# Induced attention with a max-out layer: quadrant maxima exchanged through DRAM, and a running softmax in batches 1 to 3

## The chip, the core and the metric

The kernel runs on one core of a Trainium2 chip. A core has five engines with instruction streams of their own: TensorE (PE in the profile, its weight loads PEld), VectorE (DVE), ScalarE (ACT), GpSimd (POOL) and SyncE (SP, which issues all transfers here). They meet only at semaphores. The metric is the device time of one execution in microseconds, the median of several runs.

## The reference

Four batches of 12544 tokens with 128 channels go through two attentions with 32 inducing vectors, and then a max-out layer:

```python
    def mab(q, kv):
        s = scale * (q @ kv.transpose(0, 2, 1))
        s = s - s.max(-1, keepdims=True)
        a = np.exp(s)
        a /= a.sum(-1, keepdims=True) + 1e-09
        return a @ kv
    h = mab(I, x)                 # I: the 32 inducing vectors; h: 32 x 128 for a batch
    return mab(x, h)
    ...
    h = np.maximum(np.maximum(x @ w1, x @ w2), x @ w3)
    return (h @ w_out)
```

The first attention has 32 queries and 12544 keys: its softmax runs over all tokens of a batch, and its result `h` is needed before the second one can start on that batch.

## The kernel before

A batch's 98 tiles of 128 tokens are cut into 7 groups: group 0 with 2 tiles, groups 1 to 6 with 16 (2048 tokens). The second attention and the max-out layer work on chunks of 512 tokens, four to a full group; a chunk has six steps, one for each 128 of the 768 hidden columns. In a step, TensorE makes `pu` and `pv` (L606, L612) in `advance`, ScalarE makes the relu `ru` and the rounded `hi`, VectorE takes the maximum `h` of `pv` and `ru` (L639), GpSimd (for some steps VectorE, L642) makes the remainder `lo`, and, six steps later, `stage2` has TensorE add three products to `acc` (L662 to L664).

All engines are scheduled by hand: an instruction stands on its engine where the Python program issues it. `main` walks over the steps; in each it calls `advance`, loads the `pT` of a chunk two ahead (every sixth step), copies and stores a finished chunk, then runs what the table `plan` holds for the step, then `stage2`. `at(s, f, ...)` enters a function at step `s`. A window is the 24 steps of one group, and `s0` is its first step. `burst` enters products at `s0 + 2` and at `s0 + 15`.

While batch b goes through these windows, the first attention of batch n = b + 1 is done in between, one group at a time (batch 0's is done ahead of the steps, in `phase1_first`). For a group gi, `attend_products` (L263, in a burst) writes 32 scores for each token into a bank, the tokens spread over four quadrants of 32 partitions. So each quadrant has a maximum of its own (`mq`, L273), and the four must become one. Before, this takes three instructions: ScalarE writes `mq` into the columns of a 128x4 tile by a mask (`attend_column`, L280), TensorE multiplies it with the constant `sel` so that every partition has all four (`attend_spread`, L287), and VectorE takes the least of them (the maxima are kept negated; `attend_least`, L291) into `mneg`. Then ScalarE takes the exponentials (`attend_weights`, L297), VectorE transposes them (`attend_transpose`, L311), and in the next burst TensorE sums weighted tokens (`attend_sums`, L321) into the `acc` bank that the running chunk does not use, from where ScalarE copies them to `hg` (`attend_keep`, L334). `softmax1` enters these; its argument `wait` is `LATE` (12 steps) for groups 2 and 3.

Every group has its own maximum. At the batch's end (window 5, steps 10 to 18) the seven are joined: their least, the weights `w` of the groups, a mask `sw` (128 x 7 x 32) from `w` and `sel`, seven products of `hg` with the mask (`combine_groups`, L423), the sum of the exponentials by a product (`total_sums`, L439), its reciprocal, and `hT`, the result.

The tiles `xTs` (group 0) and `xT` hold transposed tokens for the score products; `load_channels` loads them on SP. SP works in order: a transfer whose data or buffer isn't ready holds up all that follow it.

Of the kernel before, what the change touches and what calls it, by code (L numbers as in the profile page):

```python
# [25 lines left out]
def kernel(ctx, tc, x, xt, ind_t, w1, w2, w3, w_out, out):  # L26
    nc = tc.nc
# [42 lines left out]
    op = ctx.enter_context(tc.tile_pool(name="op", bufs=2))  # L70
    ps = ctx.enter_context(tc.tile_pool(name="ps", bufs=1, space=PSUM))
# [152 lines left out]
    def start_batch(b):  # L224
        st = state[b] = {"xT": {}, "xg": {}, "a": {}, "s": {}}
        st["mneg"] = bp.tile([P, NG], F32, name="mneg", tag="mneg")
        st["lst"] = bp.tile([P, NG], F32, name="lst", tag="lst")
        st["hg"] = bp.tile([P, NG, C], F32, name="hg", tag="hg", bufs=1)
# [63 lines left out]

    def attend_weights(b, gi):
        w = groups[gi]["nt"] * M
        st = state[b]
        a = wk.tile([P, 512], F32, name="a", tag="a")
        nc.scalar.activation(  # L297
# [3 lines left out]
            bias=st["mneg"][:, gi : gi + 1],  # L301
            accum_out=st["lst"][:, gi : gi + 1],
        )
        st["a"][gi] = a
# [24 lines left out]
    def attend_keep(b, gi):  # L329
# [4 lines left out]
        nc.scalar.copy(out=st["hg"][:parts, gi, :], in_=st["h"][:parts, :C])  # L334

# [388 lines left out]
    for b in range(B):  # L724
        base = b * per_batch + short
        n = b + 1
        for g in range(1, NG):
# [7 lines left out]
            if n < B:  # L735

                if g == 1:
                    at(s0, start_batch, n)
                    at(s0, load_channels, n, 0)
                    at(s0, load_channels, n, 1)  # L740
                    if n == 1:
                        at(s0 + 1, load_tokens, 1, 4)
# [4 lines left out]
                    at(s0 + 16, attend_keep, n, 0)  # L747
# [3 lines left out]
                elif g < NG - 2:  # L751
                    first += [(attend_sums, n, g - 1), (attend_products, n, g, bank_a[1])]
                    at(s0 + 3, attend_keep, n, g - 1)
# [7 lines left out]
                    if g == NG - 3:  # L761
                        second += [(attend_sums, n, g), (attend_products, n, g + 1, bank_a[1])]
                        at(s0 + 16, attend_keep, n, g)
                        softmax1(n, g + 1, s0 + 15)
                        at(s0 + 16, load_tokens, n + 1, 2)
                elif g == NG - 2:
                    first += [(attend_sums, n, g), (attend_products, n, g + 1, bank_a[1])]
                    at(s0 + 3, attend_keep, n, g)
# [137 lines left out]
```

## Time and profile before

| What | Value |
|---|---|
| median of 3 runs | 843.36 us |
| lowest and highest run | 843.27 and 845.08 us |
| the profiled execution's span, first to last instruction | 841.7 us |
| what lies around it, to the median of the runs | 1.7 us |
| mean granted TensorE clock | 0.995 |
| busy share of the span | PE 97%, ACT 88%, DVE 75%, POOL 75% |

A row of the groups or of the timeline reads: line, engine, operation, tiles written <- read, shape, number of instructions. In the timeline the start and the length stand ahead, and in brackets the idle time of the engine before it with what ended it. Lengths of TensorE instructions are modelled and overlap; their starts are what counts. The span leaves out what the device does around the program, so that it can be a little under the time of a run; the page gives no other time for the profiled execution.

### The profile page before, as it was taken

The page shows a single profiled execution, that of the slowest core. Times are in us where ns is not written, and L with a number is a line of the kernel's source. Part 1 is how long each engine was busy: PE and PEld are TensorE (multiplying, and loading weights), DVE is VectorE, ACT ScalarE, POOL GpSimd, SP SyncE. Part 2 cuts the span into 40 slices and gives each one's busy share as a digit, 9 for nine tenths or more (in the row PEclk, how much of TensorE's full clock was granted, in tenths as well). Part 3 has the DMA queues.
Part 4 walks back from the last instruction along what each step waited for, and adds up shares of the span by engine and source line. Part 5 has one row for each costly group of instructions (what it writes and reads, how often), then busy time and mean ns, then how long its engine had stood idle before and what let it go on. Part 6 is the DMA issues. An engine that isn't in the chain of part 4 may idle for free.

```text
span 841.7 us, 14677 instructions
## 1 busy us (share of the span) xinstructions
PE 817.0 (97%) x4608; PEld 635.9 (76%) x4608; DVE 630.7 (75%) x1076; ACT 741.3 (88%) x1547; POOL 635.4 (75%) x512
## 2 busy tenths in 40 slices
PE   6879999999999999999999999999999999999998
PEld 4647778777787777777777777877768878778786
DVE  5868778777686777777787778777868778777864
ACT  5759889898798998988799889889879999999996
POOL 0039778778597787877778878878759888888887
PEclk9989999999999999999999999999999999999999
DMA  9734624433425345244332462432222222222221
GB/s 348 267 96 155 219 76 157 169 116 103 146 66 175 126 157 173 70 164 158 114 92 76 162 216 70 163 122 58 64 77 81 79 75 69 64 70 76 72 79 51
DMA packets 42717, 102.50 MB, mean 122 GB/s; under 512 B 8976, under 2 KB 11152, under 8 KB 37392
## 3 DMA queue, kind: packets, MB, share of 16 engines
q1 hardware_dynamic: 42640, 101.57, 37.3%
q8 instruction: 37, 0.61, 0.3%
q14 instruction: 40, 0.33, 0.1%
HBM read 48.12 MB, written 25.69 MB: 88 GB/s over the span
## 4 chain that ended last, share of the span: by engine, by line
PE 92%; DMA 3%; DVE 2%; ACT 1%; issue 1%; SPq 0%; ACTq 0%; DVEq 0%
PE acc L662 17%; PE acc L663 16%; PE acc L664 16%; PE pu L606 16%; PE pv L612 16%; PE acc L661 3%; PE aux L525 3%; PE acc L321 2%; DMA xg<-in_x_dram 2%; PE aux L263 2%; DMA xTs<-in_xt_dram 1%; PE aux L490 1%; PE aux L423 1%; ACT ru L621 0%; PE acc L287 0%
## 5 line engine op out<-in xcount | busy, mean ns | idle before, releaser
L636 POOL TENSOR_TENSOR lo<-h,hi 128x512 fp32r<-128x512 f32 (+1 forms) x498 | 629.5, 1296 | 153.6 <-ACT hi L628 100.5
L639 DVE TENSOR_TENSOR h<-pv,ru 128x512 f32<-128x512 f32 (+1 forms) x600 | 404.5, 675 | 188.0 <-PE pv L612 122.6
L621 ACT ACTIVATE ru<-pu 128x512 f32<-128x512 f32 (+1 forms) x600 | 375.8, 626 | 73.8 <-PE pu L606 70.7
L628 ACT CAST hi<-h 128x512 fp32r<-128x512 f32 (+1 forms) x600 | 386.9, 645 | 0.3 <-DVE h L639 0.3
L662 PE MATMUL acc<-hi,wo_hi 128*128 128x512 f32 (+1 forms) x600 | 238.4, 397 | 0.0
L606 PE MATMUL pu<-pT,us 128*128 128x512 f32 (+1 forms) x600 | 232.7, 388 | 3.4 <-ACT hi L628 1.2
L612 PE MATMUL pv<-pT,us 128*128 128x512 f32 (+1 forms) x600 | 233.4, 389 | 0.0
L663 PE MATMUL acc<-hi,wo_lo 128*128 128x512 f32 (+1 forms) x600 | 232.0, 387 | 0.0
L664 PE MATMUL acc<-lo,wo_hi 128*128 128x512 f32 (+1 forms) x600 | 231.8, 386 | 0.0
L662 PEld LDWEIGHTS acc<-hi,wo_hi 128*128 128x128 f32 x600 | 113.2, 189 | 43.0 <-issue 22.0
L606 PEld LDWEIGHTS pu<-pT,us 128*128 128x128 f32 x600 | 113.2, 189 | 26.9 <-POOL us L479 2.0
L612 PEld LDWEIGHTS pv<-pT,us 128*128 128x128 f32 x600 | 113.4, 189 | 23.8 <-DVE h L639 1.3
L664 PEld LDWEIGHTS acc<-lo,wo_hi 128*128 128x128 f32 x600 | 113.0, 188 | 23.0
L663 PEld LDWEIGHTS acc<-hi,wo_lo 128*128 128x128 f32 x600 | 113.3, 189 | 20.6
L642 DVE TENSOR_TENSOR lo<-h,hi 128x512 fp32r<-128x512 f32 x102 | 72.4, 710 | 0.8 <-ACT hi L628 0.8
L669 ACT COPY o<-acc 128x512 f32<-128x512 f32 (+1 forms) x100 | 61.6, 616 | 3.1 <-PE acc L664 3.1
L661 PE MATMUL acc<-pT,us 128*128 128x512 f32 (+1 forms) x100 | 38.7, 387 | 0.0
L321 PEld LDWEIGHTS acc<-xg,aT 128*32 128x32 f32 x768 | 20.5, 110 | 13.9 <-ACT ru L621 5.7
L219 POOL TENSOR_TENSOR wo_lo<-wf,wo_hi 128x768 fp32r<-128x768 f32 x1 | 1.8, 1809 | 37.5 <-ACT wo_hi L218 37.5
L263 PE MATMUL aux<-xT,iT 128*32 128x512 f32 x192 | 25.9, 596 | 1.6 <-ACT xT L255 1.6
L321 PE MATMUL acc<-xg,aT 128*32 128x128 f32 x768 | 25.8, 274 | 1.5 <-DVE aT L311 1.1
L525 PE MATMUL aux<-xT,hT 128*32 128x512 f32 x192 | 25.6, 604 | 0.0
(101 smaller groups left out, 438.6 us busy)
## 6 DMA issues: line engine op xcount, KB each, us to landing
out_dram<-o SPq DMA_DIRECT2D x96, 256.0 KB, 2.0
xg<-in_x_dram SPq DMA_DIRECT2D x23, 1024.0 KB, 7.3
xT<-in_xt_dram SPq DMA_DIRECT2D x18, 1024.0 KB, 5.3
pT<-ph SPq DMA_DIRECT2D x192, 64.0 KB, 2.0
pT<-pl SPq DMA_DIRECT2D x192, 64.0 KB, 2.0
raw<-in_w_dram SPq DMA_DIRECT2D x3, 768.0 KB, 12.0
us<-uh SPq DMA_DIRECT2D x6, 208.0 KB, 3.1
us<-ul SPq DMA_DIRECT2D x6, 208.0 KB, 3.7
```

The lines of the kernel that those rows point to most:

```text
L321: nc.tensor.matmul(out=hps[q * M : (q + 1) * M, :C], lhsT=aT[:, t * M : (t + 1) * M], rhs=xg[:, t, :], start=(t < NQ), stop=(t + NQ >= nt),)
L606: nc.tensor.matmul(out=pu[:, :w], lhsT=state[c.b]["us"][:, 2 * j * P : (2 * j + 1) * P], rhs=c.pT[:, :w], start=True, stop=True)
L612: nc.tensor.matmul(out=pv[:, : d.w], lhsT=state[d.b]["us"][:, (2 * j + 1) * P : (2 * j + 2) * P], rhs=d.pT[:, : d.w], start=True, stop=True,)
L621: nc.scalar.activation(out=ru[:, :w], in_=pu[:, :w], func=AF.Relu)
L628: nc.scalar.copy(out=hi[:, : c.w], in_=h[:, : c.w])
L636: nc.gpsimd.tensor_sub(**args)
L639: nc.vector.tensor_max(out=h[:, : d.w], in0=pv[:, : d.w], in1=relus.pop(s)[:, : d.w])
L642: nc.vector.tensor_sub(**low)
L661: nc.tensor.matmul(out=c.acc[:, :w], lhsT=us[:, 2 * DF :], rhs=c.pT[:, :w], start=True, stop=False)
L662: nc.tensor.matmul(out=c.acc[:, :w], lhsT=wo_hi[:, j, :], rhs=c.hh[j][:, :w], start=False, stop=False)
L663: nc.tensor.matmul(out=c.acc[:, :w], lhsT=wo_lo[:, j, :], rhs=c.hh[j][:, :w], start=False, stop=False)
L664: nc.tensor.matmul(out=c.acc[:, :w], lhsT=wo_hi[:, j, :], rhs=c.hl[j][:, :w], start=False, stop=(j == NJ - 1))
```

## The change

In batches 1 to 3 the four quadrants' maxima go through DRAM: `attend_send` writes `mq` to a small DRAM tile `mqd`, `attend_fetch` reads it back so that every partition has the four values of its inducing vector, in `mm`. `running_least` takes the least of these four and of the least so far. `attend_weights` uses that running maximum as its bias, and makes the factor `fac` by which what was summed before must shrink; `running_sums` keeps one running tile `hs` and one running sum `ls` on VectorE. At the end `running_totals` makes two products with `sel`, in place of the seven products and the mask. Everything from the exponentials on stands one step later in `softmax1`; the products and sums stay in their bursts. And `start_batch` and the first two loads of batches 2 and 3 move from the first step of the window in which they are used to steps 8 and 14 of the window before. Batch 0 stays as it was.

```diff
+    def attend_send(b):
+        st["md"] = dp.tile([P], F32, name="mqd", tag="mqd")
+        nc.sync.dma_start(out=st["md"].rearrange("(m q) -> q m", q=NQ), in_=st["mq"])
+    def attend_fetch(b, gi):
+        every = st["md"].rearrange("(m q) -> m q", q=NQ).unsqueeze(0).to_broadcast([NQ, M, NQ])
+        nc.sync.dma_start(out=st["mm"][:, gi, :NQ], in_=every)
+    def running_least(b, gi):
+        known = NQ + 1 if gi > 0 else NQ
+        nc.vector.tensor_reduce(
+            out=st["mm"][:, gi + 1, NQ:], in_=st["mm"][:, gi, :known], axis=AX.X, op=ALU.min
+        )
...
     def attend_weights(b, gi):
+        least = st["mneg"][:, gi : gi + 1] if b == 0 else st["mm"][:, gi + 1, NQ:]
...
+        if b > 0 and gi > 0:
+            nc.scalar.activation(
+                out=st["fac"][:, gi : gi + 1], in_=st["mm"][:, gi, NQ:], func=AF.Exp, bias=least, scale=-1.0
+            )
...
+    def running_sums(b, gi):
+        if gi == 0:
...
+            nc.vector.tensor_copy(out=st["hs"][:parts, :], in_=st["h"][:parts, :C])
+            return
+        nc.vector.scalar_tensor_tensor(
+            out=st["hs"], in0=st["hs"], scalar=fac, in1=st["h"][:, :C], op0=ALU.mult, op1=ALU.add
+        )
+        nc.vector.scalar_tensor_tensor(out=st["ls"], ...)   # the same for the sum of the exponentials
+    def running_totals(st, bank):
+        st["lp"], st["sum"] = bank[:, :M], bank[:, M : 2 * M]
+        nc.tensor.matmul(out=st["lp"], lhsT=st["ls"].to_broadcast([P, P]), rhs=sel[:, :M], start=True, stop=True)
+        nc.tensor.matmul(out=st["sum"], lhsT=st["hs"], rhs=sel[:, :M], start=True, stop=True)
...
     def softmax1(b, gi, s, wait=0):
         at(s + 2, attend_max, b, gi)
-        at(s + 3, attend_column, b)
-        at(s + 6 + wait, attend_spread, b)
-        at(s + 7 + wait, attend_least, b, gi)
-        at(s + 8 + wait, attend_weights, b, gi)
-        at(s + 10 + wait, attend_transpose, b, gi)
+        at(s + 3, attend_send, b)
+        at(s + 4, attend_fetch, b, gi)
+        at(s + 8 + wait, running_least, b, gi)
+        at(s + 9 + wait, attend_weights, b, gi)
+        at(s + 11 + wait, attend_transpose, b, gi)
...
-                    at(s0 + 10, combine_least, ("state", n))
-                    at(s0 + 11, combine_weights, ("state", n))
-                    at(s0 + 14, combine_mask, ("state", n))
-                    at(s0 + 16, attend_keep, n, g + 1)
-                    at(s0 + 15, sum_groups, ("state", n))
+                    at(s0 + 16, running_sums, n, g + 1)
-                    at(s0 + 16, total_sums, ("state", n))
-                    at(s0 + 17, combine_groups, ("state", n), range(NG), bank_a[1])
-                    at(s0 + 17, invert_total, ("state", n))
+                    at(s0 + 18, running_totals, ("state", n), bank_a[1])
+                    at(s0 + 18, invert_total, ("state", n))
...
+                    if n + 1 < B:
+                        at(s0 + 8, start_batch, n + 1)
+                        at(s0 + 8, load_channels, n + 1, 0)
+                        at(s0 + 14, load_channels, n + 1, 1)
```

Elsewhere `attend_keep` becomes `running_sums` at the same step. Three places show what the instructions' order becomes. In the changed kernel's own lines, L699 is the maximum `h` (L639 before), L702 the `lo` (L642), L343 the transposition (L311), L316 the running least.

VectorE of batch 2's group 1, from the step before the burst whose sums read `aT`, before:

```order
L639 TENSOR_TENSOR h<-pv_83,ru 128x512
L639 TENSOR_TENSOR h<-pv_84,ru 128x512
L642 TENSOR_TENSOR lo<-h,hi 128x512
L311 STREAM_TRANSPOSE aT<-a 128x512
L639 TENSOR_TENSOR h<-pv_83,ru 128x512
L642 TENSOR_TENSOR lo<-h,hi 128x512
L639 TENSOR_TENSOR h<-pv_84,ru 128x512
L538 STREAM_TRANSPOSE aux_79<-aux_79 128x512
```

and now:

```order
L699 TENSOR_TENSOR h<-pv_85,ru 128x512
L699 TENSOR_TENSOR h<-pv_86,ru 128x512
L702 TENSOR_TENSOR lo<-h,hi 128x512
L699 TENSOR_TENSOR h<-pv_85,ru 128x512
L702 TENSOR_TENSOR lo<-h,hi 128x512
L343 STREAM_TRANSPOSE aT<-a 128x512
L699 TENSOR_TENSOR h<-pv_86,ru 128x512
L598 STREAM_TRANSPOSE aux_81<-aux_81 128x512
L378 SCALAR_TENSOR_TENSOR hs<-hs,fac,acc_87 128x128
L381 SCALAR_TENSOR_TENSOR ls<-lst,fac 128x1
```

The transposition moved behind one more maximum and one more `lo`, and the running sums stand behind the next transposition of scores.

TensorE at the end of batch 2, before (L439 is the product of the sums, L423 those with the mask):

```order
L612 MATMUL pv_83<-pT,us 128x512
L439 MATMUL acc_85<-sel,l_5211 128x32
L662 MATMUL acc_86<-hi,wo_hi 128x512
L663 MATMUL acc_86<-hi,wo_lo 128x512
L664 MATMUL acc_86<-lo,wo_hi 128x512
L606 MATMUL pu_81<-pT,us 128x512
L612 MATMUL pv_84<-pT,us 128x512
L423 MATMUL aux_80<-sw,hg 128x64 x7
L662 MATMUL acc_86<-hi,wo_hi 128x512
```

and now, at the step after the later of the two:

```order
L672 MATMUL pv_85<-pT,us 128x512
L393 MATMUL aux_82<-sel,ls 128x32
L394 MATMUL aux_82<-sel,hs 128x32
L721 MATMUL acc_87<-pT,us 128x512
L722 MATMUL acc_87<-hi,wo_hi 128x512
```

Two small products stand where there were eight, and in a bank of the scores (`aux`) instead of one of `acc`.

SP for group 6 of batch 2, before (L91 loads tokens of the next batch, L670 stores a finished chunk, L591 loads `pT`):

```order
L91 DMA xg<-in_x_dram 128x2048
L670 DMA out_dram<-o 128x512
L591 DMA pT<-ph 32x512
L591 DMA pT<-pl 32x512
L591 DMA pT<-ph 32x512
```

and now (L304 sends, L310 fetches):

```order
L304 DMA mqd<-mq 4x32x1
L92 DMA xg<-in_x_dram 128x2048
L730 DMA out_dram<-o 128x512
L310 DMA mm<-mqd 128x1x4
L651 DMA pT<-ph 32x512
```

The send stands ahead of the large load and holds it until the maxima are there; the fetch stands behind it.

More of the change, by code (lines that the diff above doesn't have):

```diff
@@ L70 @@
     op = ctx.enter_context(tc.tile_pool(name="op", bufs=2))
+    dp = ctx.enter_context(tc.tile_pool(name="dp", bufs=2, space=bass.MemoryType.DRAM))
     ps = ctx.enter_context(tc.tile_pool(name="ps", bufs=1, space=PSUM))
@@ L225, in start_batch @@
         st = state[b] = {"xT": {}, "xg": {}, "a": {}, "s": {}}
-        st["mneg"] = bp.tile([P, NG], F32, name="mneg", tag="mneg")
         st["lst"] = bp.tile([P, NG], F32, name="lst", tag="lst")
-        st["hg"] = bp.tile([P, NG, C], F32, name="hg", tag="hg", bufs=1)
+        if b == 0:
+            st["mneg"] = bp.tile([P, NG], F32, name="mneg", tag="mneg", bufs=1)
+            st["hg"] = bp.tile([P, NG, C], F32, name="hg", tag="hg", bufs=1)
+        else:
+            st["mm"] = bp.tile([P, NG + 1, NQ + 1], F32, name="mm", tag="mm")
+            st["fac"] = bp.tile([P, NG], F32, name="fac", tag="fac")
+            st["hs"] = bp.tile([P, C], F32, name="hs", tag="hs")
+            st["ls"] = bp.tile([P, 1], F32, name="ls", tag="ls")
     def start_group(b, gi):
@@ L300, in attend_weights @@
             func=AF.Exp,
-            bias=st["mneg"][:, gi : gi + 1],
+            bias=least,
             accum_out=st["lst"][:, gi : gi + 1],
         )
+        if b > 0 and gi > 0:
+            nc.scalar.activation(
+                out=st["fac"][:, gi : gi + 1], in_=st["mm"][:, gi, NQ:], func=AF.Exp, bias=least, scale=-1.0
+            )
         st["a"][gi] = a
@@ L334, in attend_keep @@
         nc.scalar.copy(out=st["hg"][:parts, gi, :], in_=st["h"][:parts, :C])
+    def running_sums(b, gi):
+        st = state[b]
+        if gi == 0:
+            parts = min(groups[gi]["nt"], NQ) * M
+            if parts < P:
+                nc.gpsimd.memset(st["hs"][parts:, :], 0.0)
+            nc.vector.tensor_copy(out=st["hs"][:parts, :], in_=st["h"][:parts, :C])
+            return
+        fac = st["fac"][:, gi : gi + 1]
+        nc.vector.scalar_tensor_tensor(
+            out=st["hs"], in0=st["hs"], scalar=fac, in1=st["h"][:, :C], op0=ALU.mult, op1=ALU.add
+        )
+        nc.vector.scalar_tensor_tensor(
+            out=st["ls"],
+            in0=st["ls"] if gi > 1 else st["lst"][:, :1],
+            scalar=fac,
+            in1=st["lst"][:, gi : gi + 1],
+            op0=ALU.mult,
+            op1=ALU.add,
+        )
+    def running_totals(st, bank):
+        st["lp"], st["sum"] = bank[:, :M], bank[:, M : 2 * M]
+        nc.tensor.matmul(out=st["lp"], lhsT=st["ls"].to_broadcast([P, P]), rhs=sel[:, :M], start=True, stop=True)
+        nc.tensor.matmul(out=st["sum"], lhsT=st["hs"], rhs=sel[:, :M], start=True, stop=True)
     def phase1_first(weights):
@@ L737 @@
                 if g == 1:
[L738 to L740 removed]
                     if n == 1:
+                        at(s0, start_batch, n)
+                        at(s0, load_channels, n, 0)
+                        at(s0, load_channels, n, 1)
                         at(s0 + 1, load_tokens, 1, 4)
```

11 lines of the change are left out of this document (7 added, 4 removed).

## The prediction

> **What bounds the kernel.** I read the page's first two parts and its chain, then the waits, then the timeline of single steps.
>
> ```profile
> span 841.7 us, 14677 instructions
> PE 817.0 (97%) x4608; PEld 635.9 (76%) x4608; DVE 630.7 (75%) x1076; ACT 741.3 (88%) x1547; POOL 635.4 (75%) x512
> PEclk9989999999999999999999999999999999999999
> PE 92%; DMA 3%; DVE 2%; ACT 1%; issue 1%; SPq 0%; ACTq 0%; DVEq 0%
> ```
>
> TensorE is busy for 97% of the span, its granted clock is 0.9 or more in all slices but one, and 92% of the chain that ends last is its own work. So a TensorE instruction that disappears is worth its whole place, a wait of TensorE costs its whole length, and work of another engine costs nothing until TensorE waits for it. The waits say the same:
>
> ```profile
> DVE h L639 <- PE pv L612: 122.6, 191, 2.7
> PE aux L263 <- DMA xTs<-in_xt_dram: 2.9, 2, 1.5
> ```
>
> VectorE waits for TensorE 191 times. The second row is one of the few waits of TensorE: twice, it stands idle for the small tile of the next batch.
>
> **Gain 1, the spreads.** Each of 21 groups (7 in each of batches 1 to 3) loses its product with `sel`, L287. In TensorE's timeline:
>
> ```profile
> 115.18 0.40 PE L612 MATMUL pv<-pT,us 128*128 128x512 f32 x1
> 115.41 0.28 PE L287 MATMUL acc<-md,sel 128*128 128x4 f32 x2
> ...
> 115.87 0.39 PE L663 MATMUL acc<-hi,wo_lo 128*128 128x512 f32 x1
> ...
> 116.55 0.39 PE L612 MATMUL pv<-pT,us 128*128 128x512 f32 x1
> ...
> 117.00 0.39 PE L663 MATMUL acc<-hi,wo_lo 128*128 128x512 f32 x1
> ```
>
> From L612 to L663 it is 0.69 us with the spread and 0.45 without it (starts are compared, since the modelled ends overlap). 0.24 x 21 = 5.0 us.
>
> **Gain 2, the end of a batch.** Seven products with the mask become one, and the product of the sums moves beside it:
>
> ```profile
> 409.75 0.39 PE L612 MATMUL pv<-pT,us 128*128 128x512 f32 x1
> 411.27 0.41 PE L439 MATMUL acc<-sel,l 128*128 128x32 f32 x2 [1.13 <-ACT hg L334]
> ...
> 411.82 0.39 PE L663 MATMUL acc<-hi,wo_lo 128*128 128x512 f32 x1
> ...
> 412.52 0.39 PE L612 MATMUL pv<-pT,us 128*128 128x512 f32 x1
> 412.75 1.67 PE L423 MATMUL aux<-sw,hg 128*128 128x64 f32 x14
> 414.23 0.48 PE L662 MATMUL acc<-hi,wo_hi 128*128 128x512 f32 x1
> ```
>
> One 512-column product takes 0.23 of start to start. The seven products take 414.23 - 412.52 - 0.23 = 1.48; the pair L439 takes 411.82 - 411.27 - 0.23 = 0.32, and I price the new product with `hs` the same. 3 x (1.48 - 0.32) = 3.5 us. L439 also waits 411.27 - 409.75 - 0.23 = 1.29 us for ScalarE's copy `hg`, because its bank holds the last sums. The new totals go to another bank, two steps (some 2.3 us) behind the vector sums that they read, so I count the whole wait as gone: 3 x 1.29 = 3.9 us. What is late next there is `hs`, which needs only the last sums and one vector turn; below nothing isn't possible, and the other end is the old wait back (0 us).
>
> **Gain 3, the loads.** `xTs` and the first `xT` of batches 2 and 3 go out in the window before instead of at the step that uses them. The row above gives 2.9 us; nothing else is read there, so the wait goes whole (other end: 0).
>
> Gains: 5.0 + 3.5 + 3.9 + 2.9 = 15.3 us.
>
> **Cost 1, the transposition comes into the step of its user.** All work behind the maximum moves one step later (`s + 10` to `s + 11`), but the sums that read `aT` stay. For the two groups of a batch whose maximum starts at `s0 + 15` (groups 1 and 5), the old transposition stood in the step before the burst and already was just too late; now it is in the burst's own step. TensorE in a window whose sums don't wait, then in one of these two, then VectorE and ScalarE there, and last the group of a small exponential:
>
> ```profile
> 323.97 1.07 PE L525 MATMUL aux<-xT,hT 128*32 128x512 f32 x8
> 324.85 1.06 PE L321 MATMUL acc<-xg,aT 128*32 128x128 f32 x32
> ...
> 292.36 1.07 PE L525 MATMUL aux<-xT,hT 128*32 128x512 f32 x8
> 293.49 1.08 PE L321 MATMUL acc<-xg,aT 128*32 128x128 f32 x32
> ```
>
> ```profile
> 292.04 0.68 DVE L642 TENSOR_TENSOR lo<-h,hi 128x512 fp32r<-128x512 f32 x1
> 292.64 0.70 DVE L311 STREAM_TRANSPOSE aT<-a 128x512 f32<-128x512 f32 x1
> 293.27 0.65 DVE L639 TENSOR_TENSOR h<-pv,ru 128x512 f32<-128x512 f32 x1
> ```
>
> ```profile
> 289.61 0.69 ACT L297 ACTIVATE a<-aux,mneg 128x512 f32<-128x512 f32 x1
> ...
> 290.29 0.60 ACT L621 ACTIVATE ru<-pu 128x512 f32<-128x512 f32 x1
> ...
> 291.75 0.63 ACT L621 ACTIVATE ru<-pu 128x512 f32<-128x512 f32 x1
> ```
>
> ```profile
> L407 ACT ACTIVATE w<-mneg,mmin 128x7 f32<-128x7 f32 x4 | 1.4, 350 | 0.0
> ```
>
> The sums start 0.88 us behind the scores where nothing is late, and 1.13 here: a wait of 0.25. In the new order the maximum of 293.27 and one more `lo` stand ahead of the transposition, 0.60 each by the starts 292.04 and 292.64. The exponential (0.68 by the starts 289.61 and 290.29) and the new factor (0.35 by L407, the nearest small exponential) now stand right ahead of the relu of 291.75, whose result that maximum reads; what they no longer delay before it gives most of this back, and about 0.1 is left. So the transposition ends some 1.3 us later and TensorE waits 1.55 in place of 0.25. Nothing covers it: VectorE can't run ahead, since its maximum needs the `pv` of the same step. 6 places x 1.3 = 7.8 us (7.2 to 9.6, if ScalarE's shift is nothing, or the whole factor and more).
>
> **Cost 2, the two late groups.** Groups 2 and 3 have twelve steps more (`LATE`); their transposition moves into the step in which groups 1 and 5 had theirs, which costs what it cost there: 0.25 x 6 = 1.5 us (0 at best).
>
> **Cost 3, the exchange.** No row shows a transfer of 128 four-byte pieces. The nearest rows, a load in 128 pieces of 128 bytes, a store to DRAM, a load between small tiles behind a large load, and two large loads with no other ahead:
>
> ```profile
> iT<-in_ind_t_dram SPq DMA_DIRECT2D x1, 16.0 KB, 1.6
> ...
> out_dram<-o SPq DMA_DIRECT2D x1, 256.0 KB, 2.0
> ...
> xT<-in_xt_dram SPq DMA_DIRECT2D x1, 1024.0 KB, 5.6
> ...
> pT<-ph SPq DMA_DIRECT2D x2, 64.0 KB, 5.0
> ...
> xg<-in_x_dram SPq DMA_DIRECT2D x1, 1024.0 KB, 4.9
> ...
> xg<-in_x_dram SPq DMA_DIRECT2D x1, 1024.0 KB, 7.9
> ```
>
> I take 2.0 us for each of the two, the store's, as the send goes to DRAM and its landing releases the fetch (1.6 to 3.0 each). Group 1 of batch 2, with no load ahead:
>
> ```profile
> 282.88 0.68 DVE L273 TENSOR_REDUCE mq<-aux 128x1 f32<-128x512 f32 x1
> ...
> 288.91 0.69 DVE L639 TENSOR_TENSOR h<-pv,ru 128x512 f32<-128x512 f32 x1 [0.34 <-PE pv L612]
> ```
>
> ```profile
> 284.10 0.34 SPq L670 DMA_DIRECT2D out_dram<-o  x1
> ```
>
> The maxima are there at 283.56, but SP's store of 284.10 is ahead, so the send goes out at 284.44, lands at 286.4, and the fetch lands at 288.4. The running minimum comes behind the maximum of 288.91, at 289.5. It is hidden with 1.1 us to spare, and VectorE's being late by up to about 1 us more would still be taken by the two `pv` banks. Behind the blocked SP stand only `pT` loads, some eight steps early, and group loads a window early: nothing.
>
> At 15 of the 21 places there is no `LATE`; at five of these (groups 0, 4, 6 of batch 1, 4 and 6 of batch 2) a megabyte load stands ahead, and a small transfer behind one lands only after it (the 5.0 us of `pT` beside the 5.6 of `xT`). Group 6 of batch 2:
>
> ```profile
> 395.40 0.67 DVE L273 TENSOR_REDUCE mq<-aux 128x1 f32<-128x512 f32 x1
> ...
> 402.14 0.68 DVE L639 TENSOR_TENSOR h<-pv,ru 128x512 f32<-128x512 f32 x1
> ```
>
> The maxima come at 396.07, and 0.4 later for the new vector sums ahead of them (0 to 0.67, that row's own length). The send goes out at 396.5; the `xg` that waited behind it on SP at 397.0; it lands 4.9 to 7.9 later, the fetch just behind it, at 402.2 to 405.2. The minimum's turn is 402.7: in time, or 2.5 late. Between 0 and 2.5 I take 0.5 at each of the five, since the slack of 1 us comes off: 2.5 us (0 to 10). The vector sums and the factor themselves are off the chain: ScalarE loses two small instructions a group for one, VectorE has the 122.6 us of waits.
>
> **Sum.** 15.3 - 7.8 - 1.5 - 2.5 = 3.5 us less. Against the profiled span of 841.7 that is 838.2; the median of the runs lies 1.7 us above that span, so 839.9 us.
>
> **What a page says against it.** The Trainium skill, "DMA: Bandwidth & Descriptors", section "Specifications", says that a transfer in pieces under 512 bytes makes the DMA engines read, modify and write; and its section "Why a DMA increments its semaphore by 16 and not by 1" says that a copy is split over the largest number of engines, 16 at most, that divides both sides' slowest dimension. By the second the send, 4x32 pieces, runs on 4 engines and not on 16. No row of this case shows either; with one more of the 0.8 us that the Trainium skill gives, in its section "Latency and other measured facts", for the shortest round trip to HBM (an estimate), the send would land at 287.2 in the example above, and the sum would stay. Only several such trips one behind the other would undo it.
>
> **Rivals.** First, the exchange is slow: small pieces, some written into the same lines of DRAM, land later than any row above. The point from which it decides: send and fetch together over 5.1 us (289.5 - 284.44) stop VectorE, over about 6.1 us TensorE. At 7 us it is 0.9 us at 15 places, 13.5 us: 853, slower than before. Against it speaks that the 128 pieces of `iT` took 1.6 us. The Trainium skill's rule on pieces under 512 bytes would work this way. Second, cost 1 doesn't come, because ScalarE and VectorE have made up time by then: 839.9 - 7.8 = 832. The wait of 0.25 that is there already speaks against it. Third, the megabyte loads land as late as 7.9 at all five places, about 2 us each: 847; at half of them, or with gain 3 lost, 842 to 845. The row of 7.9 stands beside one of 4.9 for the same load, so either can be.
>
> **How the numbers follow.** 0.2% (1.7 us) is about what can be told from no change. The forecast, 836 to 841.6: 0.54. The second rival, 829 to 835: 0.14. Faster together: 0.68. Half of the third, within 0.2%: 0.13. Slower: the exchange 0.13, all five loads 0.06, together 0.19. The range from 831 to 849 leaves out the far half of the second rival and most of the first.
>
> **What would show it.** Right: no L287 for batches 1 to 3; L423 gone there; `aux<-xTs` starts about 0.9 us behind the scores; sums of groups 1 and 5 start about 2.4 us behind them, those of 2 and 3 1.1; the send and the fetch land in 2 us where no load is ahead. Wrong: waits of VectorE for `mm` at the 15 places followed by TensorE's on `h`; a totals product that waits for `hs`; or sums that start 0.9 to 1.2 us behind the scores.

## The result and the profile after

The changed kernel takes 1010.95 us (median of four runs, 1009.3 to 1012.0) against 844.22 us of the kernel before beside it. The ratio is 1.197, with a 95% interval of 1.195 to 1.199: 20% slower, where 839.9 us and at most 849 were forecast. The page of the changed kernel, in the lines that were shown of before:

```profile
span 1007.5 us, 14691 instructions
PE 859.9 (85%) x4530; PEld 651.8 (65%) x4530; DVE 642.8 (64%) x1103; ACT 749.4 (74%) x1520; POOL 641.5 (64%) x512
PEclk9998799988899879988889997898988999999999
PE 57%; DMA 28%; DVE 8%; ACT 3%; issue 2%; POOL 1%; SPq 0%; DVEq 0%; ACTq 0%; POOLq 0%
```

TensorE has 78 instructions fewer and is yet busy for 42.9 us more (859.9 against 817.0); the clock row shows why, with 7s and 8s in batches 1 to 3, where it stood at 9. The rest is idleness: 1007.5 - 859.9 = 147.6 us against 24.7. Both together are the 165.8 us by which the span grew. In the chain that ends last, transfers now have 28% instead of 3%. The waits name them:

```profile
DVE h L699 <- PE pv L672: 150.0, 204, 5.8
DVE mm L316 <- DMA mm<-mqd: 115.6, 15, 10.6
PE pv L672 <- DVE h L699: 91.8, 18, 8.9
ACT o L729 <- DMA out_dram<-o: 38.1, 7, 7.3
```

The second row is the one that the prediction gave as its sign of being wrong: VectorE waits for the fetched maxima at 15 places, the 21 without the six `LATE` ones, 7.7 us each. TensorE's wait for `h` is its echo. The fourth is new too: output stores land so late that ScalarE has no free buffer.

One place in detail, group 1 of batch 1, with no load ahead. First SP's timeline (start, length, the transfer issued), then VectorE's and TensorE's there, last the clock by stretches (busy time by engine, `PEclk`, share of the transfer engines, GB/s):

```profile
93.66 0.59 SPq L304 DMA_DIRECT2D mqd<-mq  x1
101.57 0.57 SPq L310 DMA_DIRECT2D mm<-mqd  x1
```

```profile
108.51 0.16 DVE L316 TENSOR_REDUCE mm<-mm 128x1 f32<-128x5 f32 x1 [10.03 <-DMA mm<-mqd]
```

```profile
100.69 0.39 PE L666 MATMUL pu<-pT,us 128*128 128x512 f32 x1
109.37 0.79 PE L672 MATMUL pv<-pT,us 128*128 128x512 f32 x1 [8.28 <-DVE h L699]
```

```profile
92.00:101.00 9.00, 9.00 (x41) 7.18 (x39) 5.33 (x9) 8.12 (x16) 7.95 (x6) 1.00 0.12 32
101.00:109.40 8.40, 0.12 (x2) 0.04 (x1) 0.89 (x3) 0.70 (x3) 0.00 (x0) 0.70 0.62 175
109.40:113.00 3.60, 3.15 (x21) 1.01 (x25) 2.93 (x5) 2.26 (x6) 1.26 (x1) 0.50 0.23 73
```

The send (L304) goes out at 93.66, and the fetch (L310), which SP may issue only when the send has landed, at 101.57: 7.9 us for 512 bytes. It is 11.1 us at the first of the 21 places and 6.8 to 9.5 at the others. Another 6.9 us pass until VectorE has the values; TensorE is out of work for 8.28 us, and afterwards its clock is granted at 0.50, so that a product of 0.39 us takes 0.79. The Trainium skill, "TensorE: Matmul & The Clock Gate", section "Part 1: The HAM clock gate (the "warmup" mystery)", says that an idle window of about 3.4 us halves TensorE's clock until it has been busy as long. The stretches above agree as to the halving (0.70 on average over the idle stretch, 0.50 behind it); in the next 5 us the average was 0.84.

### The profile page after: what moved, and what is told of

Same layout as the page of the kernel before. It is cut to its first block, busy times and chain, and to the rows that moved or that the text cites. A ratio compares the mean times of both kernels' runs of the same rounds, so it can differ in the third digit from the quotient of the medians.

```text
span 1007.5 us, 14691 instructions
## 1 busy us (share of the span) xinstructions
PE 859.9 (85%) x4530; PEld 651.8 (65%) x4530; DVE 642.8 (64%) x1103; ACT 749.4 (74%) x1520; POOL 641.5 (64%) x512
## 4 chain that ended last, share of the span: by engine, by line
PE 57%; DMA 28%; DVE 8%; ACT 3%; issue 2%; POOL 1%; SPq 0%; DVEq 0%; ACTq 0%; POOLq 0%
DMA mqd<-mq 13%; PE acc L722 10%; PE pv L672 10%; PE pu L666 9%; PE acc L723 9%; PE acc L724 9%; DMA out_dram<-o 8%; DMA mm<-mqd 7%; DVE h L699 3%; PE acc L353 3%; PE aux L270 2%; PE aux L585 2%; PE acc L721 1%; POOL lo L696 1%; ACT ru L681 1%
## 5 line engine op out<-in xcount | busy, mean ns | idle before, releaser
L699 DVE TENSOR_TENSOR h<-pv,ru 128x512 f32<-128x512 f32 (+1 forms) x600 | 401.8, 674 | 220.2 <-PE pv L672 150.0
L681 ACT ACTIVATE ru<-pu 128x512 f32<-128x512 f32 (+1 forms) x600 | 365.0, 608 | 94.4 <-PE pu L666 89.3
L688 ACT CAST hi<-h 128x512 fp32r<-128x512 f32 (+1 forms) x600 | 375.8, 626 | 5.9 <-DVE h L699 5.3
L672 PE MATMUL pv<-pT,us 128*128 128x512 f32 (+1 forms) x600 | 244.3, 407 | 92.1 <-DVE h L699 91.8
L666 PE MATMUL pu<-pT,us 128*128 128x512 f32 (+1 forms) x600 | 239.1, 399 | 36.3 <-ACT ru L681 33.0
L723 PE MATMUL acc<-hi,wo_lo 128*128 128x512 f32 (+1 forms) x600 | 237.9, 397 | 0.0
L724 PE MATMUL acc<-lo,wo_hi 128*128 128x512 f32 (+1 forms) x600 | 236.5, 394 | 0.0
L724 PEld LDWEIGHTS acc<-lo,wo_hi 128*128 128x128 f32 x600 | 116.8, 195 | 24.7
L325 ACT ACTIVATE a<-aux,mm 128x512 f32<-128x512 f32 (+1 forms) x21 | 13.3, 636 | 90.7 <-DVE mm L316 90.7
L702 DVE TENSOR_TENSOR lo<-h,hi 128x512 fp32r<-128x512 f32 x102 | 74.3, 728 | 4.6 <-PE acc L724 3.1
L316 DVE TENSOR_REDUCE mm<-mm 128x1 f32<-128x5 f32 (+1 forms) x21 | 3.3, 155 | 115.6 <-DMA mm<-mqd 115.6
L353 PE MATMUL acc<-xg,aT 128*32 128x128 f32 x768 | 30.9, 311 | 5.8 <-DVE aT L343 5.4
L270 PE MATMUL aux<-xT,iT 128*32 128x512 f32 x192 | 30.9, 698 | 1.6 <-ACT xT L262 1.6
```

Of the source, the lines that this page charges most:

```text
L353: nc.tensor.matmul(out=hps[q * M : (q + 1) * M, :C], lhsT=aT[:, t * M : (t + 1) * M], rhs=xg[:, t, :], start=(t < NQ), stop=(t + NQ >= nt),)
L666: nc.tensor.matmul(out=pu[:, :w], lhsT=state[c.b]["us"][:, 2 * j * P : (2 * j + 1) * P], rhs=c.pT[:, :w], start=True, stop=True)
L672: nc.tensor.matmul(out=pv[:, : d.w], lhsT=state[d.b]["us"][:, (2 * j + 1) * P : (2 * j + 2) * P], rhs=d.pT[:, : d.w], start=True, stop=True,)
L681: nc.scalar.activation(out=ru[:, :w], in_=pu[:, :w], func=AF.Relu)
L688: nc.scalar.copy(out=hi[:, : c.w], in_=h[:, : c.w])
L699: nc.vector.tensor_max(out=h[:, : d.w], in0=pv[:, : d.w], in1=relus.pop(s)[:, : d.w])
```

## The experiments

The theory at first was that the loss is the wait for the send's landing and nothing else. The rivals: the fetch is slow as well, the other edits cost more than priced, or the send hinders other transfers.

**No send.** The send returns at once, and the fetch reads a constant:

```diff
-        nc.sync.dma_start(out=st["md"].rearrange("(m q) -> q m", q=NQ), in_=st["mq"])
+        return
-        every = st["md"].rearrange("(m q) -> m q", q=NQ)...
+        every = ind_t[:M, :NQ]...
```

> Leaves out the first of the two transfers: the second one reads a constant of the inputs instead of the quadrant maxima, in the same 16-byte pieces, and so waits for nothing; the weights are scaled by a wrong maximum. Everything else stays as in the changed kernel. Theory A (the landing of the first transfer, 6.8 to 9.5 us instead of the 2.0 us that the prediction took, is the cause of the whole loss; all other terms stand): about 840 us, 836 to 845, and VectorE's wait for mm nearly gone. Rival B (the other edits cost too: transposition and weights late, running sums on VectorE): above 855 us. Rival C (the fetch is slow as well, 2.5 us and more): VectorE still waits 1 us or more at most of the 15 places, 845 to 855 us.

843.92 us against 843.84 (ratio 0.9998, 0.9982 to 1.0014). So the 167.0 us between this run and the changed kernel hang on one transfer of 512 bytes. VectorE waits for `mm` once only, for 0.7 us, so the fetch by itself is fast enough. But 840 was expected, so some other term was wrong by 4 us as well; the runs further down find it.

**Send issued, nobody reads it.** Only the second half of that diff:

> Both transfers are issued where the changed kernel issues them, but the second reads a constant of the inputs, so nothing waits for the first to land (the weights are scaled by a wrong maximum). Theory A (only the wait for the landing costs): within 2 us of the run without the first transfer. Rival D (the first transfer also holds up what stands behind it in the queues: the fetch itself and the output stores, whose late landing ScalarE waited 38.1 us for in the changed kernel): 10 to 40 us above the run without it, with VectorE still waiting for mm or ScalarE for the output buffers.

984.27 us (1.166, 1.1642 to 1.1678). The first theory falls: the wait for the landing is worth 26.7 us, and 140.4 us are left when nothing waits for it. The waits of this run:

```profile
DVE mm L316 <- DMA mm<-in_ind_t_dram: 88.5, 15, 9.6
ACT o L729 <- DMA out_dram<-o: 43.7, 7, 8.1
```

The fetch of a constant, whose data is there from the start, now reaches VectorE 8 to 15 us behind the send, where the real one took 10 to 16, and it was in time without the send. So the send holds up what is issued behind it.

**Send issued, no fetch at all.** To see whether that is only the exchange's own fetch, the fetch was left out and the minimum taken over zeros:

```diff
+            nc.gpsimd.memset(st["mm"], 0.0)
-        at(s + 4, attend_fetch, b, gi)
```

> The first transfer is issued as in the changed kernel, the second is left out, and the minimum is taken over zeros that lie in SBUF, so that nothing waits for either (the weights are not scaled by a maximum). With both transfers issued and the first unread, VectorE still waited 88.5 us for the second to land and ScalarE 43.7 us for output stores, and the time was 984.3 us; with no send 843.9 us. Theory D1 (the 140 us between are mostly the late second transfer, that is waits of the exchange's own chain): 850 to 890 us, the remaining loss being output stores that land late. Rival D2 (the sends hold up the kernel's other transfers as much): above 900 us, with ScalarE's wait for the output buffers or others grown past 45 us. Rival D3 (the stores were late only since all was late): 842 to 848 us.

946.62 us (1.1164, 1.1097 to 1.123), above the 900 of D2:

```profile
ACT o L730 <- DMA out_dram<-o: 76.3, 15, 8.9
PE pu L667 <- ACT ru L682: 71.0, 14, 8.4
PE pu L667 <- DMA pT<-pl: 7.4, 4, 2.5
```

It is 102.7 us above the run without a send (the kernel before took 845.05 beside it, 1.2 us more than beside that run). So some 100 us of the loss come from transfers that carry nothing of the exchange: the output stores, which ScalarE and then TensorE wait for, and a few `pT` loads.

**The send on another queue.** In the run with the unread send, ScalarE issues it instead of SP:

```diff
-        nc.sync.dma_start(out=st["md"]...
+        nc.scalar.dma_start(out=st["md"]...
```

> The run in which nobody reads the send (984.3 us), with the send issued by ScalarE on its own queue instead of SP's. If what holds up the fetch and the stores is their place behind the send in one queue: 845 to 870 us (843.9 without a send, and 21 issues on ScalarE of about 0.6 us). If it is the transfer engines or the memory that the sends occupy: it stays above 930 us.

940.59 us (1.1149, 1.1114 to 1.1184). A queue of its own takes away 43.7 us and leaves 96.7, so it isn't mainly the place behind the send in one queue. The Trainium skill, "DMA: Bandwidth & Descriptors", section "Queues, rings and completion order", says that the mark of a transfer's end is written only when all earlier writes of the same transfer engine have landed, those of its other queues too. By that rule one slow write makes every later transfer on its engine look unfinished, whoever issued it. The last three runs agree with a delay across queues; no trace here shows which engine moved what.

A late mark is not the whole of it, though, and the transfer engines are not busy with the send itself. In the run above, with the sends on ScalarE's queue, these have a row of their own in the page (packets, MB, share of 16 engines' span):

```profile
q10 hardware_dynamic: 2772, 0.01, 0.2%
```

In the run without a fetch, a load of 1 MB is issued at 387.16 us, right behind a send at 386.48. These are the stretches ahead of the send, behind it, and after that (columns as above):

```profile
382.00:386.00 4.00, 4.00 (x20) 3.14 (x18) 2.92 (x6) 2.87 (x6) 2.06 (x2) 1.00 0.82 279
388.00:399.00 11.00, 8.63 (x39) 6.80 (x37) 7.39 (x13) 6.93 (x15) 8.76 (x7) 1.00 0.98 36
399.00:402.00 3.00, 0.00 (x0) 0.00 (x0) 0.00 (x0) 0.00 (x0) 0.00 (x0) 0.98 0.83 319
```

For 11 us behind the send the engines are counted busy but move 36 GB/s, against 279 before and 319 after. So the data of the load itself comes late. What holds it up is not shown.

**Where the 128 pieces lie.** Four layouts of the send in one kernel, by batch:

```diff
+        if b == 1:   # 512 bytes for each inducing vector
+            nc.sync.dma_start(out=st["md"][:, :NQ].rearrange("m q -> q m"), in_=st["mq"])
+        if b == 2:   # partition order
+            nc.sync.dma_start(out=st["md"].unsqueeze(1), in_=st["mq"])
+        elif gi == 5:
+            nc.sync.dma_start(out=st["md"].rearrange("(q m) -> q m", q=NQ), in_=st["mq"])
+        else:        # four rows of 128 bytes
+            nc.vector.transpose(out=mr, in_=mqs)
+            nc.sync.dma_start(out=..., in_=mr.rearrange("(q m) c -> q m c", q=NQ)[:, 0, :])
```

> The first transfer in four layouts, to see what makes it take 8 us from its issue to the issue of the fetch that waits for it; from a quarter of batch 3 on the fetched values belong to other inducing vectors. Batch 1: the four values of an inducing vector go to a line of their own, 512 bytes apart (128 pieces of 4 bytes). Batch 2: the 128 values go to one stretch of 512 bytes in partition order (128 pieces of 4 bytes, each beside the one before). Batch 3: the column is first transposed on VectorE in blocks of 32x32, and 4 pieces of 128 bytes go out; its group 5 sends 4-byte pieces with the pieces of a quadrant side by side. Theory E (4-byte pieces that fall into the same stretch of DRAM wait for one another): batch 1 falls to about 2.5 us, batch 2 and group 5 of batch 3 stay near 8, the rows of batch 3 fall to about 2.5. Rival F (each piece costs about 0.2 us in its engine, 32 pieces one after the other): batch 1 stays near 8; a send that is spread over 16 engines falls to about 3.5; the rows fall to about 2.3. Rival G (a fixed time of the path, whatever the pieces): all stay at 7 to 9 us.

SP's timeline at group 5 of batches 1 and 2, group 1 of batch 3 (rows) and group 5 of batch 3; each pair is the send and the fetch that waits for it:

```profile
183.87 0.60 SPq L310 DMA_DIRECT2D mqw<-mq  x1
186.50 0.58 SPq L328 DMA_DIRECT2D mm<-mqw  x1
...
423.94 0.38 SPq L314 DMA_DIRECT2D mqd<-mq  x1
431.14 0.58 SPq L328 DMA_DIRECT2D mm<-mqd  x1
...
541.65 0.53 SPq L321 DMA_DIRECT2D mqd<-mr  x1
543.34 0.58 SPq L328 DMA_DIRECT2D mm<-mqd  x1
...
639.88 0.38 SPq L316 DMA_DIRECT2D mqd<-mqs  x1
647.72 0.58 SPq L328 DMA_DIRECT2D mm<-mqd  x1
```

2.6, 7.2, 1.7 and 7.8 us. Over all places: 512 bytes for each vector 2.0 to 2.8 (5.1 at the first), partition order 7.2 to 9.6, rows 1.6 to 1.7. That is theory E. 128 pieces of 4 bytes are not slow as such; they are slow when all fall into one stretch of 512 bytes. The whole kernel took 907.1 us, a mixture.

**The same pieces, apart, in all batches.** One edit to the changed kernel:

```diff
-        st["md"] = dp.tile([P], F32, name="mqd", tag="mqd")
+        st["md"] = dp.tile([M, P], F32, name="mqd", tag="mqd")
```

and the views (the fetch's too) cut to the first four of each 128.

> The changed kernel with one edit: in DRAM the four maxima of an inducing vector have 512 bytes to themselves (the tile is 32 x 512 bytes instead of 512 bytes in all); the send's 128 pieces of 4 bytes, its engines, the fetch's 128 pieces, the wait between them and all steps are as in the changed kernel. If the loss comes from pieces that share 512 bytes: 843.9 us (no send) plus the waits that batch 1 of the run with four layouts still showed (1.2, 2.0 and 3.6 us in 7 places, some 7 us a batch): 850 to 866 us. If the mere number of 4-byte pieces, or the two transfers one after the other, cost as much: above 900 us.

847.26 us (1.0046, 1.0029 to 1.0063), below the expected range. The send took 2.0 to 3.0 us (4.4 at the first place). Placing alone carries 163.7 of the 167.0 us. Number of pieces, the two transfers in a row and SP's wait between them cost the remaining 3.3 us. With this mended, the change still does not pay.

**How far apart.** Two runs on the unit, each executed once, with the send's tile as 32 rows of 64 bytes, 32 rows of 32 bytes and 128 rows of 64 bytes (one piece in each):

```diff
+            st["md"] = dp.tile([M, 16 // b], F32, ...)      # batches 1 and 2
+            st["md"] = dp.tile([M, NQ, 16], F32, ...)       # batch 3
```

> The first transfer with 128 pieces of 4 bytes each, further apart in DRAM. Batch 1: 64 bytes for each inducing vector's four values (32 pieces in 512 bytes, 4 pieces in 64 bytes). Batch 2: 32 bytes for each vector (64 pieces in 512 bytes, 8 in 64). Batch 3: every piece in 64 bytes of its own (8 in 512, 1 in 64). The send took 2.0 to 2.8 us with 4 pieces in 512 bytes, and 6.8 to 9.5 us with 128. If pieces in the same 512 bytes wait for one another (some 50 ns each): about 3.5 us in batch 1, 5 us in batch 2, 2.3 us in batch 3. If the unit is 64 bytes: near 2.3 us in all three. If only adjacent pieces meet: 7 to 9 us in batches 1 and 2 still, since four stand side by side.

2.1 to 3.1, 3.9 to 4.7 and 2.0 to 2.5 us (the first send of the kernel, 5.7, aside); the whole kernel took 856.98 us. This is nearest to the first of the three patterns, pieces in the same 512 bytes. Then runs of 16, 32 and 64 pieces side by side, each run in 512 bytes of its own:

```diff
+        n = 8 * 2**b
+        st["md"] = dp.tile([P // n, P], F32, ...)
+        nc.sync.dma_start(out=st["md"][:, :n], in_=st["mq"])
```

> The changed kernel's send with its 128 pieces of 4 bytes side by side in runs, each run at the start of 512 bytes of its own: in batch 1 eight runs of 16 pieces (64 bytes), in batch 2 four runs of 32 (128 bytes), in batch 3 two runs of 64 (256 bytes). The fetch waits for the send as before, but brings the first four values to all (wrong maxima). Pieces so far per 512 bytes and send times: 4 and 8: 2.0 to 2.8 us, 32: 2.1 to 3.2, 64: 3.9 to 4.7, 128: 6.8 to 9.6; per 64 bytes the same layouts have 4, 1, 4, 8 and 16 pieces, so both units fit. If the unit is 512 bytes (61 ns a piece, 2.0 at least): about 2, 2 and 4 us. If it is 64 bytes: about 8 us in all three. If 128 or 256 bytes: 4, 8, 8 or 2, 4, 8.

Group 1 of batch 2 and group 5 of batch 3 of the second run:

```profile
302.25 0.60 SPq L305 DMA_DIRECT2D mqw<-mq  x1
306.29 0.58 SPq L313 DMA_DIRECT2D mm<-mqw  x1
...
685.41 0.59 SPq L305 DMA_DIRECT2D mqw<-mq  x1
695.34 0.59 SPq L313 DMA_DIRECT2D mm<-mqw  x1
```

Runs of 16 took 2.4 to 4.5 us (5.9 at the first place), of 32 4.0 to 6.4, of 64 9.9 to 11.2. The whole kernel took 965.46 us. None of the four patterns came as it was named; 2, 4, 8 is the nearest. 64 pieces in 256 bytes took longer than 128 in 512, and per piece of a run the two rows give 0.13 and 0.16 us (4.04 for 32, 9.93 for 64) against 0.06 (7.8 us for 128) before. Fixed units of 64 or 128 bytes that work side by side are out, since a run of 32 pieces would fill one and take as long as the full 512 bytes. But the number of runs changes with their length here (8, 4 and 2), so the two can't be told apart. The size of the unit, and why the price of a piece differs, stay open.

**The old exchange with the rest of the change.** Column, product and minimum at the old steps; running minimum by one more instruction on VectorE; the rest as changed:

```diff
+        nc.vector.tensor_reduce(out=now, in_=st["mp"][:, :NQ], axis=AX.X, op=ALU.min)
+        if gi > 0:
+            nc.vector.tensor_tensor(out=now, in0=now, in1=st["mm"][:, gi, NQ:], op=ALU.min)
```

> The old exchange (column, product by sel, minimum over the four columns, at the old steps) with the rest of the change: running minimum (one more small VectorE instruction), running sums, one product per batch, moved loads of xTs. Theory A: the gains of batch end, hg wait and moved loads stand (3.5 + 3.9 + 2.9 us), 18 small extra minima cost about 1 us: about 834 us, 831 to 838. Rival B (running sums or the moved loads cost as much as they bring): 841 to 846 us.

839.73 us (0.9948, 0.9935 to 0.9961): a gain, 5.7 us short of the expected one, between the ranges of theory A and rival B. The next three runs take the terms apart.

**The moved loads alone.** The hunk on `start_batch` and `load_channels`, put into the kernel before:

> The kernel before with the moved loads of xTs (and of the first xT of the next batch) as the only edit. The prediction's third gain stands: 2.9 us less, about 841 us. Rival: the wait for xTs was covered by other work, or the loads now stand in the way of others: within 1 us of before, 843 to 845 us.

841.84 us (0.997, 0.9958 to 0.9983): 2.0 us of the 2.9.

**Without the products.** That kernel, without column and product, the minimum over a constant:

```diff
-        at(s + 3, attend_column, b)
-        at(s + 6 + wait, attend_spread, b)
+        at(s + 4, attend_constant, b, gi)
```

> The kernel before with the moved loads and, in batches 1 to 3, without the column scalings and the 21 products that spread them; the minimum is taken over a constant that one transfer brings, at the old steps (the weights are scaled by a wrong maximum); groups' sums are kept and combined at the end of the batch as before. Against the moved loads alone (841.8 us) it measures the first gain: 5.0 us by the prediction, so about 837 us. What then lies between it and the run without the first transfer at early steps (835.2 us) is the second gain: 7.4 us by the prediction, less what the running sums cost. If the first gain is 5.0 the second can be no more than 2; if the second is whole, the first is near 0 and this run stays near 842 us.

837.37 us (0.9917, 0.9902 to 0.9931): 4.5 us less than the moved loads alone, of 5.0.

**No send, old steps.** The run without a send, with minimum, weights and transposition a step earlier:

```diff
-        at(s + 8 + wait, running_least, b, gi)
+        at(s + 7 + wait, running_least, b, gi)
...
-        at(s + 11 + wait, attend_transpose, b, gi)
+        at(s + 10 + wait, attend_transpose, b, gi)
```

> The run without the first transfer, with minimum, weights and transposition back at the steps of before (s + 7, 8, 10). The second transfer reads a constant, as there; the weights are scaled by a wrong maximum. If the prediction's costs 1 and 2 (7.8 us for the transposition in the burst's own step, 1.5 us at the late groups) are right, it is 9.3 us faster than that run: about 834.5 us. Rival: the costs were overpriced, and the gains with them: 838 to 842 us. Against the run with the old exchange (839.7 us), which has the 21 products spread over the quadrants and the column scalings and is otherwise alike, it shows the first gain: 5.0 us by the prediction.

835.16 us (0.9901, 0.9884 to 0.9918): 8.8 us less than at the later steps, where 9.3 were expected. Its distance to the run with the old exchange, 4.6 us, is a second measure of the first gain. Its distance to the run without products, 2.2 us, is what the second gain brings net of the running sums; the intervals of these two runs are some 1.3 us either way.

**The exchange mended.** The rows landed in 1.7 us, so the whole exchange was done with rows, from SBUF to SBUF:

```diff
+        nc.vector.transpose(out=rows, in_=mqs)
+        four = rows.rearrange("(q m) c -> q m c", m=M)[:, 0, :]
+        for r in range(NQ):
+            nc.sync.dma_start(out=quads[r * M : r * M + NQ, :], in_=four)
...
+        nc.vector.transpose(out=cols, in_=quads)
+        nc.vector.tensor_reduce(out=now, in_=cols[:, :NQ], axis=AX.X, op=ALU.min)
+        if gi > 0:
+            nc.vector.tensor_tensor(out=now, in0=now, in1=st["mm"][:, gi, NQ:], op=ALU.min)
```

> The exchange mended: the column of quadrant maxima is transposed on VectorE in blocks of 32x32, the four rows of 128 bytes go from SBUF to the four quadrants of another tile in SBUF (four transfers of four pieces, no DRAM), a second transposition makes them columns, and minimum, weights and transposition stand at the steps of before; running minimum, running sums, one product per batch and moved loads as in the changed kernel. Theory (pieces of 128 bytes land in about 2 us, and the first gain of 5.0 us is real): 835 us, 833 to 838, and VectorE doesn't wait for the rows. Rival H (the first gain is as overpriced as the others turned out): 837 to 840 us. Rival I (four more issues on the queue, or the landing, hold something up): above 841 us.

839.34 us (0.995, 0.9934 to 0.9966), the time that rival H had named. VectorE waited 0.6 us in all for the rows. Its groups show something else (us busy, mean ns, us idle before):

```profile
L320 DVE TENSOR_TENSOR mm<-mm 128x1 f32<-128x1 f32 x18 | 12.8, 709 | 0.6
```

and the one just ahead of it, by its tile (count, lengths in ns, first and last start):

```profile
L318 DVE TENSOR_REDUCE mm<-cols x21: 156/157/159, 72.8 to 600.1; 128x1 f32<-128x4 f32 x21
```

The minimum of two columns takes 709 ns on average, more than four times the reduction of four columns whose result it reads. The run with the old exchange has this minimum too, at half the length:

```profile
L318 DVE TENSOR_TENSOR mm<-mm 128x1 f32<-128x1 f32 x18 | 6.3, 352 | 0.6
```

Why it is longer beside the transpositions is not shown. One reduction over five columns replaced both, with the transposed columns written beside the running minimum:

```diff
-            nc.vector.tensor_tensor(out=now, in0=now, in1=st["mm"][:, gi, NQ:], op=ALU.min)
+        nc.vector.transpose(out=st["mm"][:, gi, 1:], in_=quads)
+        nc.vector.tensor_reduce(out=st["mm"][:, gi + 1, :1],
+            in_=st["mm"][:, gi, 0 if gi else 1 : 1 + NQ], axis=AX.X, op=ALU.min)
```

> The mended exchange by rows again, but the running minimum stands beside the transposed columns, so that one reduction takes the four maxima and it together (as in the changed kernel). In the run before it the separate minimum of two columns took 709 ns each, 18 times, 12.8 us of VectorE. If these are why that run was no faster than the old exchange (839.3 against 839.7 us): 835 to 837 us, near the 835.2 us of the run that sends nothing. If it is the two small transpositions or the four issues on the queue: 838 to 840 us still.

835.54 us (0.9897, 0.988 to 0.9914), the 835 to 837 expected. It leaves nothing out, is 1% faster than the kernel before, and lies 0.4 us from the run that sends nothing: this exchange is nearly hidden. In its profile one wait stands out that the run without a send doesn't have, 1.8 us of ScalarE for a `pT` load; whether the exchange makes that load late was not run.

## Why the prediction was wrong, step by step

Single traces check the medians. The rows are TensorE's `pu` of all 600 steps: count, lengths in ns, first and last start in us. The difference of the two starts leaves out batch 0's first attention ahead of the steps, which is the same in all these kernels and yet took 50.1 to 53.8 us.

The kernel before:

```profile
L606 PE MATMUL pu<-pT,us x600: 277/390/764, 50.2 to 831.7; 128*128 128x512 f32 x144, 128*128 128x256 f32 x6
```

The moved loads alone:

```profile
L606 PE MATMUL pu<-pT,us x600: 277/389/767, 52.5 to 830.8; 128*128 128x512 f32 x144, 128*128 128x256 f32 x6
```

Without the products:

```profile
L616 PE MATMUL pu<-pT,us x600: 277/389/763, 50.3 to 823.7; 128*128 128x512 f32 x144, 128*128 128x256 f32 x6
```

No send, old steps:

```profile
L665 PE MATMUL pu<-pT,us x600: 277/389/767, 52.6 to 823.8; 128*128 128x512 f32 x144, 128*128 128x256 f32 x6
```

No send:

```profile
L665 PE MATMUL pu<-pT,us x600: 277/389/764, 53.8 to 834.2; 128*128 128x512 f32 x144, 128*128 128x256 f32 x6
```

The same pieces, apart:

```profile
L666 PE MATMUL pu<-pT,us x600: 277/389/763, 50.1 to 835.2; 128*128 128x512 f32 x144, 128*128 128x256 f32 x6
```

The changed kernel:

```profile
L666 PE MATMUL pu<-pT,us x600: 277/389/796, 53.0 to 997.3; 128*128 128x512 f32 x144, 128*128 128x256 f32 x6
```

In this order 781.5, 778.3, 773.4, 771.2, 780.4, 785.1 and 944.3 us.

| Term | Forecast | By the medians | By the steps |
|---|---|---|---|
| gain 1, spreads | 5.0 | 4.5 | 4.9 |
| gain 2, batch end, net | 7.4 | 2.2 | 2.2 |
| gain 3, loads | 2.9 | 2.0 | 3.2 |
| costs 1 and 2, a step later | 9.3 | 8.8 | 9.2 |
| cost 3, exchange | 2.5 | 167.0 | 163.9 |

**Cost 3** is the step that failed, twice. Its price came from the wrong row: "I take 2.0 us for each of the two, the store's, as the send goes to DRAM". That store moves 256 KB to places of its own; the send's 128 pieces share 512 bytes and took 6.8 to 9.5 us (11.1 at the first). The first rival had the mechanism ("written into the same lines of DRAM"), and its point of decision was right: with send and fetch together above 6.1 us, TensorE stops. But it was priced at 7 us, where 10 to 16 came, and was given 0.13, on the strength of `iT`'s 128 pieces in 1.6 us. Those are a load, of 128 bytes each, and say nothing about small writes side by side. The second failure is one of scope, in the prediction and in the rival: both count only the exchange's own chain ("Behind the blocked SP stand only `pT` loads"). More than half of the loss (some 100 us) also comes when nobody waits for the exchange, because the kernel's own loads and stores then land late, and a wait of TensorE costs a second time by the halved clock. The rule on pieces under 512 bytes that the prediction takes from the Trainium skill ("DMA: Bandwidth & Descriptors", section "Specifications") was set aside there as a matter of 0.8 us; read as a cost for each piece, it would have led here. Read so it is too wide, since the same pieces 512 bytes apart are also under 512 bytes and cost 3.3 us in the whole kernel.

**Costs 1 and 2** were right to 0.5 us, within the noise. In the run without a send, sums of group 2 of batch 2, then of group 5, against the scores ahead of them:

```profile
327.25 1.06 PE L584 MATMUL aux<-xT,hT 128*32 128x512 f32 x8
328.38 0.86 PE L352 MATMUL acc<-xg,aT 128*32 128x128 f32 x24
...
392.67 1.06 PE L584 MATMUL aux<-xT,hT 128*32 128x512 f32 x8
395.15 1.08 PE L352 MATMUL acc<-xg,aT 128*32 128x128 f32 x32 [1.41 <-DVE aT L342]
```

1.13 and 2.48 us, where the prediction had named 1.1 and 2.4. So its second rival (cost 1 doesn't come) is out.

**Gains 1 and 3** came nearly whole. **Gain 2** came whole at its own place, and most of it was lost again elsewhere: 2.2 of 7.4 us were left. Here are the starts of `pu` at steps 17 and 20 of window 5, where batch 2's totals are made, in the run without products and then in the run without a send at old steps:

```profile
404.88 0.40 PE L616 MATMUL pu<-pT,us 128*128 128x512 f32 x1
...
411.75 0.39 PE L616 MATMUL pu<-pT,us 128*128 128x512 f32 x1
```

```profile
407.53 0.39 PE L665 MATMUL pu<-pT,us 128*128 128x512 f32 x1
...
411.62 0.39 PE L665 MATMUL pu<-pT,us 128*128 128x512 f32 x1
```

These three steps take 6.87 and 4.09 us, 2.8 less, and the other two batches have the same; 2.5 for each batch were forecast. The waits for `hg` did go, and the totals wait for nothing. The loss is in other steps of the same two traces. VectorE has a wait in the second that the first doesn't have:

```profile
DVE lo L701 <- PE acc L723: 2.7, 3, 0.9
```

It stands early in window 1 of batches 1 to 3, and steps 6 and 7 there take about 1 us more each time, 3 us in all. While batch 3 goes through its windows no first attention is left and no vector sums run, so they can't be the cause there; which edit is, stays open. Most of the rest, again some 3 us, is in small pieces behind the groups' exponentials. ScalarE's timeline in the second run, at step 13 of window 4, shows what stands there:

```profile
367.66 0.22 ACT L324 ACTIVATION_READ_ACCUMULATOR a<-aux,mm 128x1 f32 x1
367.75 0.31 ACT L332 ACTIVATE fac<-mm 128x1 f32<-128x1 f32 x1
367.94 0.61 ACT L680 ACTIVATE ru<-pu 128x512 f32<-128x512 f32 x1
```

The factor stands ahead of the relu for 0.19 us, in a stretch where ScalarE works without a pause, and this step and the next three take 0.4 us more than in the run without products. So the sentence "The vector sums and the factor themselves are off the chain" doesn't hold for the factor. How much is the factor's and how much the vector sums' was not run apart.

**What follows for the sum.** With the measured terms 1 to 3 and costs 1 and 2 the change without its exchange is worth next to nothing (843.92 against 843.84; 1.1 us by the steps), not 6 us. With an exchange nearly as cheap as forecast (the pieces apart, 3.3 us for 2.5) it is 0.5% slower, so "faster" would have been wrong even then.

## What to carry to other kernels

Price a small transfer by a row of the same kind (direction, piece size, and whether pieces share a stretch of DRAM), and where there is none, let the range reach to a serial cost for each piece. Ask of a slow transfer not only who waits for it but what is issued behind it: here the late stores and loads of the rest of the kernel cost more than the wait for the slow transfer itself. For an exchange across partitions, turn the column into rows on VectorE first and send those, and fold a running minimum into the reduction that is there anyway.

## What the runs showed of the hardware

- 128 writes of 4 bytes into one stretch of 512 bytes of DRAM took 6.8 to 9.6 us until a dependent transfer could be issued (the first of a kernel aside); 512 bytes apart by four 2.0 to 3.0; as four rows of 128 bytes 1.6 to 1.7.
- A pending write of this kind delayed transfers that don't depend on it, from the same queue and from another (984.3 and 940.6 us against 843.9 without it). A load of 1 MB behind one moved at 36 GB/s for 11 us, and at 319 after that.
- After a wait of 8.28 us TensorE's granted clock was 0.50 for the next 3.6 us.
- A VectorE minimum of two 128x1 columns, right behind the reduction that writes one of them, took 709 ns on average in one kernel and 352 in another; the reduction of four columns took 157 and 151.
